# Turning keys and queries by VectorE block transposes and DMAs through DRAM, from step 13 on, in a DeltaNet and hardswish kernel

## The chip, the cores and the metric

The kernel runs on one core of a Trainium2 chip. The metric is the time of one execution in microseconds (us) on the device. A core has five engines that each work through a queue of their own in order: TensorE (PE; its weight loads are listed apart as PEld), VectorE (DVE), ScalarE (ACT), GpSimd (POOL) and SyncE (SP, which here only sends DMAs). They wait for each other by semaphores.

## The reference

Two stages. The first is a recurrence over 768 tokens for 4 batches and 8 heads of width 48, the second a two-layer network over the 3072 rows that come out of it. All is in float32.

```python
def _attn_ref(q, k, v, beta):                     # (4, 8, 768, 48)
    k_n = k / (np.linalg.norm(k, axis=-1, keepdims=True) + 1e-06)
    state = zeros((B, H, D, D))
    for t in range(S):
        y[:, :, t] = einsum('bhd,bhde->bhe', q[:, :, t], state)
        v_old = einsum('bhde,bhd->bhe', state, k_n[:, :, t])
        state = state + beta[:, :, t] * einsum('bhd,bhe->bhde', k_n[:, :, t], v[:, :, t] - v_old)
    return y
def _moe_ref(x, w_in, w_out):                     # (3072, 384), (384, 2048), (2048, 384)
    h = x @ w_in
    g = h * np.clip(h + 3.0, 0.0, 6.0) / 6.0
    return g @ w_out
```

## The kernel before

**Chunks and steps.** The 768 tokens are cut into N = 24 chunks of C = 32. A tile of 128 partitions holds one chunk of all four batches (32 rows a batch). Each chunk t is one step of the recurrence, and has three kinds of work:

- The preparation `prep(t)`: GpSimd multiplies the keys by their inverse norms (`kb`, L510). TensorE turns keys and queries, four 128x128 transposes each, into PSUM (`pt`, L524), in which heads lie two by two, padded from 48 to 64 columns. ScalarE evicts them into one tile (`KQ`, L532) that has the head's width along the partitions. GpSimd makes a mask (`mb`, L486). TensorE multiplies keys by keys and queries (`sc`, L547, 64 small matmuls), and VectorE writes the products with the mask (`L` and `LB`, L558). GpSimd scales the keys by beta (`bkb`, L498).
- The inverse of a lower triangular matrix for each chunk, for four chunks at a time, on VectorE (`A`, `pr`, L759 and L764, many short instructions; block transposes at L469 and L473).
- The chain `chain(t)`: the state times `KQ` (`ks`, L806), the residual `R` (L901, L909), `pz` and `py` (L827), the state's update (`su`, L938; `state`, L956), and the output row turned for the second stage (`yt`, L873; `xT`, L877). The chain of t + 1 needs the state of t.

**The second stage** works on blocks of two chunks (256 rows). First comes the up product with the gate: 16 units by the plain product (`ph`, L994; gate L1001 and L1004) for early blocks, or, from block 5 on, by a scheme with fewer products (`up_by_eleven`: `ph`, L1066; GpSimd's sums L1030; ScalarE's L1080, L1100, L1104; VectorE's L1093, L1097, L1107), for which VectorE first makes sums over tokens (L1056). Then comes the down product, from block 2 on with seven products in the place of eight (`po`, L1218; sums L1204; ScalarE's L1225; adds L1228), 14 units. At its end eight DMAs store the block's rows (`out_dram`, L1143).

**Order.** Every engine's order is that in which the program issues the instructions. A list by hand (`ORDER`) sets it for the start, steps 0 to 4. From step LS = 5 on, a loop does one step per turn and cuts it into 15 units. In each unit it first runs what a table `plan` holds for that unit (a piece of the chain or of a preparation), then issues `loads`, then one unit of the second stage, then some pieces of the inverse (`fill`); how many is worked out from an estimate of VectorE's load (`USED`, `CHAIN`). The second stage's 30 units per block are two steps, so the same unit of a block falls on the same place in every second step; the stores are issued in unit 11 of the odd steps. Whenever the loop is at step t, the preparation of t + 6 is being done (fewer ahead in the first two turns, called `behind`), and the one of t + 7 is begun:

```python
                1: lambda: (take(ch), take(now)),
                2: lambda: (take(ch), take(now), take(gens["q"], 4)),
                4: lambda: (take(ch), take(now)),
                5: lambda: take(now),
                6: lambda: take(now),
                13: lambda: take(later),
```

Here `now` is the preparation of t + 6 and `later` that of t + 7; `take(x)` lets it run to its next `yield`. So `kb` is made in unit 13 of the step before, the keys are turned in unit 1, the queries in unit 2, and `sc` comes in unit 4.

**SyncE's queue.** All loads and stores of these steps are sent by SyncE in program order: four `vf` loads (L193) at the beginning of a step, four `qb` loads (L180) in unit 2, two `kf` loads (L168) per unit in some steps, and the stores. Each of these has 48 KB. A send whose buffer isn't free, or whose data isn't ready, keeps all sends behind it waiting.

**Buffers.** PSUM has four banks for `pt`, `ph`, `po`, `pz`, `py` and `yt` in a ring ("pm"), and two pairs for `ks`, `su` and `sc`. There are two buffers for `kb`, four for `qb`, six for `KQ`. The tile `o` of the stores (one buffer) is also used by ScalarE's L1104.

Of the kernel before, what the change touches and what calls it, by code (L numbers as in the profile page):

```python
# [9 lines left out]
FP32 = mybir.dt.float32  # L10
# [34 lines left out]
def kernel(  # L45
# [21 lines left out]
    nc = tc.nc  # L67
# [27 lines left out]
    def rows(b):  # L95
        return slice(C * b, C * b + C)
# [20 lines left out]
    mb_spare = spares[:, 8 * H * C : 10 * H * C]  # L117
    bkb_spare = spares[:, 10 * H * C : 10 * H * C + H * DP].rearrange("p (h w) -> p h w", w=DP)
    assert 10 * H * C + H * DP == 3 * NPR * P
    kbufs = [persist.tile([P, H, DP], FP32, name=f"kb{i}") for i in range(NKB)]  # L120
    qbufs = [persist.tile([P, H, DP], FP32, name=f"qb{i}") for i in range(NQB)]
    bkbufs = [bkb_spare] + [
        persist.tile([P, H, DP], FP32, name=f"bkb{i}") for i in range(1, NBKB)
    ]
# [1 line left out]
    def bkb_of(t):  # L126
        return bkbufs[t if t < NBKB else 1 + (t - 1) % (NBKB - 1)]
# [3 lines left out]
    def tokens(ap, b, t):  # L131
        return ap[b, :, t * C : (t + 1) * C, :].rearrange("h t d -> t h d")
# [4 lines left out]
    def needs(*what):  # L137
        assert past.issuperset(what), (what, set(what) - past)
# [33 lines left out]

    def load_q(t, eng=nc.sync):
        if t < N:
            if t >= NQB:
                needs(("qT", t - NQB))
            elif t:
                needs(*pad(t))
            for b in range(B):
                eng.dma_start(out=qbufs[t % NQB][rows(b), :, 0:D], in_=tokens(q, b, t))  # L180
                if b == B - 1:
                    past.add(("q", t))
                yield
# [310 lines left out]
    def scaled(t):  # L494
        needs(("kb", t), *pad(t), *([("bkb", t - NKB)] if t >= NKB else []))
        if t >= NBKB:
            needs(("su", t - NBKB + 1))
        nc.gpsimd.tensor_tensor(  # L498
            out=bkb_of(t)[:, :, 0:D], in0=kbufs[t % NKB][:, :, 0:D],
            in1=beta_tok[:, t, 0:H].unsqueeze(2).to_broadcast([P, H, D]), op=ALU.mult,  # L500
        )
        past.add(("bkb", t))
        yield

    def prep(t, whole=True):

        g, i = group(t)
        kb, qb = kbufs[t % NKB], qbufs[t % NQB]
        needs(*([("bkb", t - NKB)] if t >= NKB else []), *(pad(t) if t < NKB and t else []))
        nc.gpsimd.tensor_tensor(  # L510
            out=kb[:, :, 0:D], in0=kfs[g][:, i],
            in1=invs.pop(t).unsqueeze(2).to_broadcast([P, H, D]), op=ALU.mult,
        )
        past.add(("kb", t))
        yield

        for j, src in enumerate((kb, qb)):
            if j == 1:
                needs(("q", t))
                past.add(("qT", t))  # L520
            ring("pm", NPM, ("pt", t, j))
            pt = psM.tile([128, NP, P], FP32, name="pt", tag=slot["pm"])
            for p in range(NP):
                nc.tensor.transpose(  # L524
                    pt[:, p, :], src[:, 2 * p : 2 * p + 2].rearrange("p e w -> p (e w)"), ident[:]
                )
# [5 lines left out]
            nc.scalar.activation(  # L532
                out=KQ[:, :, 0:4:3, :] if j == 0 else KQ[:, :, 1:3, :],
                in_=pt[:].rearrange("q p (x y c) -> q (p x) y c", y=2, c=C), func=ACTF.Copy,
            )
            if whole and j == 0:
                drain(mask(t))
            yield
        ring("pc", NPC, ("sc", t))
        sc = psC.tile([P, 2, 512], FP32, name="sc", tag=slot["pc"])  # L540
        scv = sc[:, :, 0 : NP * 2 * C].rearrange("p e (a j w) -> p e a j w", a=NP, j=2)
        for p in range(NP):
            for b in range(B):
                for e in range(2):
                    r = slice(DP * e, DP * e + DP)
                    kq = KQ[r, p * B // 2 + b // 2]
                    nc.tensor.matmul(  # L547
                        scv[rows(b), e, p],
                        lhsT=kq[:, 3 if b % 2 else 0, :],
                        rhs=kq[:, 3:1:-1, :] if b % 2 else kq[:, 0:2, :],  # L550
                        start=True, stop=True,
                    )
# [12 lines left out]
        if whole:  # L565
            drain(scaled(t))
        yield
# [219 lines left out]
    def chain(t, whole=True):  # L787
# [10 lines left out]
        def of_state():  # L798
            ph = [banks("ks", t, i) for i in range(2)]
            for p in range(NP):  # L800
                for b in (0, 2, 1, 3):
                    for e in range(2):
                        r = slice(DP * e, DP * e + DP)
# [622 lines left out]
    with tc.manual_schedule():  # L1426
# [11 lines left out]
        loads = iter(())  # L1438
        left = due = 0
        USED = {"up": 0.42, "eleven": 1.0, "down": 0.7}  # L1440
        CHAIN = {0: 0.45, 1: 0.75, 2: 0.75, 3: 0.4, 4: 0.4, 6: 0.5, 9: 0.8, 10: 0.6, 14: 0.2}
        for t in range(LS, N):
            g, i = group(t)
# [9 lines left out]
            if i == 2:  # L1453
# [12 lines left out]
                11: lambda: token_sums(t // CB),  # L1466
                13: lambda: take(later),
            }
            if behind:
                for u in (7, 8, 10, 11, 12, 13):  # L1470
                    plan[u] = lambda ch=plan.get(u): (ch and u < 13 and ch(), take(more))
                plan[14] = lambda: take(later)
            ready = (2, 0) if behind or i == 2 and t - LS == LA - LE else (1, 6)
            for u in range(NU):
                if u in plan:
                    plan[u]()
                take(loads, 2)
# [12 lines left out]
                settle(1)  # L1490
                while evicts:
                    evicts.pop(0)()
                if i == 1 == ready[0] and 5 < u < 7:
                    continue
                if i == 0 or not left:
                    take(fill, 2 if i or u < 2 else u > 4)
                    continue
                room = max(1.65 - USED[mode["of"]] - CHAIN.get(u, 0), 0.15) / mode["mean"]
                due += room * left / max((GS - i) * NU - u, 1)
                due = min(due, 2.6)  # L1500
                take(fill, int(due))
                left, due = max(left - int(due), 0), due - int(due)
# [33 lines left out]
```

## Time and profile before

| what | value |
|---|---|
| median of 3 runs | 667.27 us (665.14 to 668.17) |
| profiled execution | 672.08 us, span of its instructions 670.4 us |
| PE busy | 636.9 us, 95% |
| DVE busy | 487.2 us, 73% |
| ACT busy | 272.8 us, 41% |
| POOL busy | 203.6 us, 30% |
| granted TensorE clock, mean | 0.985 of full speed |
| memory traffic | 26.84 MB read, 4.72 MB written |

The profile is of one execution. Its page gives the busy time of each engine, the span in 40 slices, the chain of work that ended last, and the costliest groups of instructions as "line, engine, operation, out<-in, shapes, count | busy us, mean ns of one | idle time before them, and what ended it". Other views cut it by stage (windows), by line or tile, or list the instructions in order of time. The page says this of the end's chain:

```profile
PE 86%; DMA 5%; DVE 3%; SPq 2%; issue 1%; ACT 1%; POOL 0%; ACTq 0%; DVEq 0%; POOLq 0%
```

### The profile page before, as it was taken

The page shows a single profiled execution, that of the slowest core. Times are in us where ns is not written, and L with a number is a line of the kernel's source. Part 1 is how long each engine was busy: PE and PEld are TensorE (multiplying, and loading weights), DVE is VectorE, ACT ScalarE, POOL GpSimd, SP SyncE. Part 2 cuts the span into 40 slices and gives each one's busy share as a digit, 9 for nine tenths or more (in the row PEclk, how much of TensorE's full clock was granted, in tenths as well). Part 3 has the DMA queues.
Part 4 walks back from the last instruction along what each step waited for, and adds up shares of the span by engine and source line. Part 5 has one row for each costly group of instructions (what it writes and reads, how often), then busy time and mean ns, then how long its engine had stood idle before and what let it go on. Part 6 is the DMA issues. An engine that isn't in the chain of part 4 may idle for free.

```text
span 670.4 us, 26330 instructions
## 1 busy us (share of the span) xinstructions
PE 636.9 (95%) x11544; PEld 568.6 (85%) x11544; DVE 487.2 (73%) x1146; ACT 272.8 (41%) x532; POOL 203.6 (30%) x320
## 2 busy tenths in 40 slices
PE   2768899999999999999999999999999999999997
PEld 2657786776688988988989999999999999999997
DVE  4889685899545777747879847988748988556354
ACT  5887568532142232232234234235244144153250
POOL 5531022002421031364155255055042141331330
PEclk9959899999999999999999999999999999999999
DMA  7888237302041030032030020020020020010000
GB/s 171 203 193 235 59 67 186 73 6 51 15 80 32 2 72 2 3 73 37 3 68 8 3 61 14 3 62 2 3 50 2 2 49 2 17 24 2 25 1 25
DMA packets 88499, 33.27 MB, mean 50 GB/s; under 512 B 80160, under 2 KB 83232, under 8 KB 88384
## 3 DMA queue, kind: packets, MB, share of 16 engines
q1 hardware_dynamic: 88128, 31.29, 20.7%
q8 instruction: 91, 1.49, 0.9%
q10 hardware_dynamic: 256, 0.30, 0.2%
q14 instruction: 24, 0.20, 0.1%
HBM read 26.84 MB, written 4.72 MB: 47 GB/s over the span
## 4 chain that ended last, share of the span: by engine, by line
PE 86%; DMA 5%; DVE 3%; SPq 2%; issue 1%; ACT 1%; POOL 0%; ACTq 0%; DVEq 0%; POOLq 0%
PE po L1218 28%; PE ph L1066 20%; PE ph L994 15%; PE po L1154 6%; PE ks L806 3%; PE su L938 3%; PE pz L827 3%; PE py L827 3%; PE pt L524 2%; PE sc L547 2%; DMA spare<-in_moe_w_in_dram 2%; DMA kf<-in_k_dram 1%; PE yt L873 1%; DMA w_out<-in_moe_w_in_dram 1%; PE pi L684 1%
## 5 line engine op out<-in xcount | busy, mean ns | idle before, releaser
L1066 PE MATMUL ph<-xT,w_in 128*128 128x128 f32 (+1 forms) x560 | 121.4, 321 | 0.8 <-ACT KQ L532 0.6
L994 PE MATMUL ph<-xT,w_in 128*128 128x256 f32 (+1 forms) x576 | 116.6, 351 | 2.9 <-DVE g L1004 2.1
L1218 PE MATMUL po<-w_out,g 128*128 128x192 f32 x640 | 110.6, 326 | 0.0
L994 PEld LDWEIGHTS ph<-xT,w_in 128*128 128x128 f32 x576 | 94.5, 192 | 15.8 <-DVE g L1004 2.9
L1218 PEld LDWEIGHTS po<-w_out,g 128*128 128x128 f32 x640 | 104.6, 190 | 0.5
L1066 PEld LDWEIGHTS ph<-xT,w_in 128*128 128x128 f32 x560 | 91.1, 191 | 6.0 <-ACT KQ L532 0.8
L1030 POOL TENSOR_TENSOR g<-g 128x256 f32<-128x256 f32 x112 | 68.0, 608 | 83.2 <-ACT g L1080 78.8
L1218 PE MATMUL po<-spare,g 128*128 128x192 f32 x480 | 86.7, 332 | 0.0
L1218 PEld LDWEIGHTS po<-spare,g 128*128 128x128 f32 x480 | 77.2, 190 | 1.8
L1001 ACT ACTIVATE g<-ph,halves 128x256 f32<-128x256 f32 (+1 forms) x96 | 41.3, 436 | 74.9 <-PE ph L994 74.8
L1080 ACT ACTIVATE g<-ph 128x512 f32<-128x512 f32 x56 | 33.4, 597 | 82.1 <-PE ph L1066 82.1
L1228 POOL TENSOR_TENSOR o<-o,u 128x192 f32<-128x192 f32 x18 | 13.2, 733 | 175.7 <-ACT o L1225 97.2
L1204 DVE TENSOR_TENSOR g<-g 128x512 f32<-128x512 f32 x80 | 55.6, 716 | 5.6 <-PE po L1218 5.6
L759 DVE TENSOR_TENSOR pr<-A 128x30 f32<-128x30 f32 (+9 forms) x150 | 57.4, 383 | 2.8
L764 DVE TENSOR_TENSOR A<-A,pr 128x30 f32<-128x30 f32 (+9 forms) x150 | 55.7, 371 | 3.7
L1004 DVE SCALAR_TENSOR_TENSOR g<-g,ph 128x256 f32<-128x256 f32 (+1 forms) x96 | 34.8, 371 | 31.7 <-ACT g L1001 31.4
L356 ACT ACTIVATE spare<-spare,places 128x768 uint16<-128x768 uint16 (+1 forms) x56 | 52.4, 942 | 2.7 <-DMA kf<-in_k_dram 1.5
L1093 DVE TENSOR_TENSOR g<-ph,g 128x256 f32<-128x256 f32 x56 | 23.5, 420 | 38.4 <-PE ph L1066 30.9
L1225 ACT ACTIVATE o<-po 128x192 f32<-128x192 f32 x40 | 13.2, 330 | 83.2 <-PE po L1218 79.6
L510 POOL TENSOR_TENSOR kb<-kf,inv 128x384 f32<-128x384 f32 x24 | 21.3, 891 | 78.8 <-issue 42.6
L1154 PE MATMUL po<-w_out,g 128*128 128x384 f32 x128 | 45.2, 491 | 0.0
L1107 DVE SCALAR_TENSOR_TENSOR g<-o,g 128x512 f32<-128x512 f32 x56 | 40.7, 726 | 5.9 <-ACT o L1104 5.9
(141 smaller groups left out, 1010.6 us busy)
## 6 DMA issues: line engine op xcount, KB each, us to landing
kf<-in_k_dram SPq DMA_DIRECT2D x96, 48.0 KB, 2.9
qb<-in_q_dram SPq DMA_DIRECT2D x96, 48.0 KB, 2.8
vf<-in_v_dram SPq DMA_DIRECT2D x96, 48.0 KB, 2.2
out_dram<-o SPq DMA_DIRECT2D x92, 48.0 KB, 1.6
spare<-in_moe_w_in_dram SPq DMA_DIRECT2D x4, 768.0 KB, 6.0
w_out<-in_moe_w_in_dram SPq DMA_DIRECT2D x4, 768.0 KB, 6.5
w_out<-in_moe_w_out_dram SPq DMA_DIRECT2D x4, 768.0 KB, 7.3
spare<-in_moe_w_out_dram SPq DMA_DIRECT2D x4, 768.0 KB, 5.7
```

What stands on the lines that cost most here:

```text
L356: nc.scalar.activation(out=z, in_=z if n else d.bitcast(I16)[:, :, :, 3], func=func, bias=places[:, n : n + 1], scale=scale,)
L759: nc.vector.tensor_tensor(out=pv, in0=A[:, j + 1 :, j].unsqueeze(2).to_broadcast([n, w, j]), in1=A[:, j, 0:j].unsqueeze(1).to_broadcast([n ...
L764: nc.vector.tensor_tensor(out=A[:, j + 1 :, 0:j], in0=A[:, j + 1 :, 0:j], in1=pv, op=ALU.subtract)
L827: nc.tensor.matmul(ps[rows(place(b)), D * h : D * h + D], lhsT=m(h)[rows(b)], rhs=z[rows(b), D * at(h) : D * at(h) + D], start=True, stop= ...
L994: nc.tensor.matmul(ph[:, cols], lhsT=w_in[:, s, f * 128 : (f + 1) * 128], rhs=xT[:, s, cols], start=(s == 0), stop=(s == NKT - 1),)
L1001: nc.scalar.activation(out=g, in_=ph, func=ACTF.Relu, bias=half, scale=1.0 / 6.0)
L1030: nc.gpsimd.tensor_tensor(out=out, in0=a, in1=b, op=op)
L1066: nc.tensor.matmul(ph[:, n], lhsT=w, rhs=x, start=start, stop=stop, skip_group_check=True)
L1107: nc.vector.scalar_tensor_tensor(out=g, in0=r, scalar=1.0, in1=g, op0=ALU.min, op1=ALU.mult)
L1154: nc.tensor.matmul(pos[c][:], lhsT=gs[blk, f // 2][:, f % 2, c * P : (c + 1) * P], rhs=w_out[:, f, :], start=(f == 0), stop=(f == NFC - 1),)
L1204: nc.vector.tensor_tensor(out=A(f, *out, 4), in0=A(f, *a, 4), in1=A(f, *b, 4), op=op)
L1218: nc.tensor.matmul(ps[n][:], lhsT=A(f - f % 2, *a)[:, f % 2], rhs=b[:, f], start=(f == 0), stop=(f == HF - 1),)
```

## The change

From TQ = 13 on, a preparation turns keys and queries another way. VectorE transposes the 32x32 blocks of the key tile (128 partitions x 384) and of the query tile. Each result is written to a DRAM tile `kq` by four DMAs, one per batch, in rows of 32 numbers; the address does the rest of the turning. Two DMAs, one for the even and one for the odd heads, read `kq` back into `KQ`, on 48 of each 64 partitions. For this the tiles of keys and queries lie dense from step 13 on (384 columns, no padding), and the matmuls that read `KQ` (`sc` and `ks`) take 48 rows in place of 64. The results of the block transposes (`turned`) stand in the place of two of the four query buffers, so two are left for queries.

In the table the preparation's pieces move: `kb` from unit 13 to 10, the key transpose with its four writes to unit 11, the query transpose with its four writes to unit 12, the two reads and the mask to unit 1 of the next step; `sc` stays in unit 4 and what follows in unit 5. For step 13's own preparation the pieces lie in units 12 to 14 of step 6. The estimate of VectorE's load has 0.75 more in units 11 and 12 (`TURN`).

```diff
-    qbufs = [persist.tile([P, H, DP], FP32, name=f"qb{i}") for i in range(NQB)]
+    TQ, HQ = LS + 2 * LE, 2
+    qb_pair = persist.tile([P, HQ, H, DP], FP32, name="qbs")
+    qbufs = [persist.tile([P, H, DP], FP32, name=f"qb{i}")[:] for i in range(NQB - HQ)] + [
+        qb_pair[:, i] for i in range(HQ)
+    ]
+    turned = qb_pair[:].rearrange("p i h w -> p (i h w)")[:, 0 : 2 * H * D].rearrange(
+        "p (k z) -> p k z", k=2
+    )
...
     def load_q(t, eng=nc.sync):
         if t < N:
-            if t >= NQB:
-                needs(("qT", t - NQB))
+            if q_before(t) is not None:
+                needs(("qT", q_before(t)))
...
+        if t >= TQ:
+            kq = scratch.tile([H * D, B // 2, 4, C], FP32, name="kq", bufs=2)
+            for j, src in enumerate((of_key(t), of_query(t))):
+                if j == 1:
+                    needs(("q", t))
+                    past.add(("qT", t))
+                nc.vector.transpose(out=turned[:, j], in_=src.rearrange("p h w -> p (h w)"))
+                for b in range(B):
+                    nc.sync.dma_start(
+                        out=kq[:, b // 2, (3 if j == 0 else 2) if b % 2 else j, :].rearrange(
+                            "(n r) c -> r n c", r=C
+                        ),
+                        in_=turned[rows(b), j].rearrange("p (n c) -> p n c", c=C),
+                    )
+                yield
+            ring("KQ", NKQ, ("KQ", t))
+            KQ = work.tile([128, NP * B // 2, 4, C], FP32, name="KQ", bufs=NKQ)
+            for e in range(2):
+                nc.sync.dma_start(
+                    out=KQ[DP * e : DP * e + D].rearrange("d (p x) y c -> d p (x y c)", p=NP),
+                    in_=kq[:].rearrange("(p e d) x y c -> e d p (x y c)", e=2, d=D)[e],
+                )
+            drain(mask(t))
+            yield
-        for j, src in enumerate((kb, qb)):
+        for j, src in enumerate((kb, qb) if t < TQ else ()):
...
-                    r = slice(DP * e, DP * e + DP)
+                    r = slice(DP * e, DP * e + (DP if t < TQ else D))
...
+        TURN = {11: 0.75, 12: 0.75}
...
+            if first_of >= TQ:
+                plan[2] = lambda: (take(ch), take(gens["q"], 4))
+                plan[6] = lambda: None
+            if first_of + 1 >= TQ and not behind:
+                plan[10] = lambda: (take(ch), take(later))
+                plan[11] = lambda: (token_sums(t // CB), take(later))
+                plan[12] = lambda: take(later)
+                plan[13] = lambda: None
...
+                if first_of + 2 == TQ:
+                    plan[12] = plan[13] = lambda: (take(more), take(later))
+            turns = TURN if first_of + 1 >= TQ else {}
...
-                room = max(1.65 - USED[mode["of"]] - CHAIN.get(u, 0), 0.15) / mode["mean"]
+                room = max(1.65 - USED[mode["of"]] - CHAIN.get(u, 0) - turns.get(u, 0), 0.15) / mode["mean"]
```

More of the change, by code (lines that the diff above doesn't have):

```diff
@@ L119, with of_key, of_query, dense @@
     assert 10 * H * C + H * DP == 3 * NPR * P
-    kbufs = [persist.tile([P, H, DP], FP32, name=f"kb{i}") for i in range(NKB)]
-    qbufs = [persist.tile([P, H, DP], FP32, name=f"qb{i}") for i in range(NQB)]
+    kbufs = [persist.tile([P, H, DP], FP32, name=f"kb{i}")[:] for i in range(NKB)]
+    TQ, HQ = LS + 2 * LE, 2
[6 more added lines that the diff above has]
+    )
+    def of_key(t):
+        return dense(kbufs[t % NKB], t)
+    def of_query(t):
+        return dense(qbufs[t % NQB if t < TQ else t % (NQB - HQ)], t)
+    def dense(x, t):
+        if t < TQ:
+            return x[:, :, 0:D]
+        return x.rearrange("p h w -> p (h w)")[:, 0 : H * D].rearrange("p (h w) -> p h w", w=D)
+    def q_before(t):
+        slot = [s % NQB if s < TQ else s % (NQB - HQ) for s in range(t + 1)]
+        return max((s for s in range(t) if slot[s] == slot[t]), default=None)
     bkbufs = [bkb_spare] + [
@@ L179, in load_q @@
             for b in range(B):
-                eng.dma_start(out=qbufs[t % NQB][rows(b), :, 0:D], in_=tokens(q, b, t))
+                eng.dma_start(out=of_query(t)[rows(b)], in_=tokens(q, b, t))
                 if b == B - 1:
@@ L498, in scaled @@
         nc.gpsimd.tensor_tensor(
-            out=bkb_of(t)[:, :, 0:D], in0=kbufs[t % NKB][:, :, 0:D],
+            out=bkb_of(t)[:, :, 0:D], in0=of_key(t),
             in1=beta_tok[:, t, 0:H].unsqueeze(2).to_broadcast([P, H, D]), op=ALU.mult,
@@ L510, in prep @@
         nc.gpsimd.tensor_tensor(
-            out=kb[:, :, 0:D], in0=kfs[g][:, i],
+            out=of_key(t), in0=kfs[g][:, i],
             in1=invs.pop(t).unsqueeze(2).to_broadcast([P, H, D]), op=ALU.mult,
@@ L802, in of_state @@
                     for e in range(2):
-                        r = slice(DP * e, DP * e + DP)
+                        r = slice(DP * e, DP * e + (DP if t < TQ else D))
                         c = slice(2 * C * (b // 2), 2 * C * (b // 2) + 2 * C)
```

## The prediction

> **What bounds the kernel now.** I read the page first: busy shares and clock.
>
> ```profile
> PE 636.9 (95%) x11544; PEld 568.6 (85%) x11544; DVE 487.2 (73%) x1146; ACT 272.8 (41%) x532; POOL 203.6 (30%) x320
> ...
> PEclk9959899999999999999999999999999999999999
> ```
>
> TensorE is busy 95% of the span, at full granted clock after the start. A busy share is a mean over stages, so next the busy time step by step, in windows cut at each step's first `ks` matmul (us from the span's start; then length, PE, PEld, DVE, ACT, POOL).
>
> ```profile
> 342.20:368.00 25.80, 25.20 (x467) 22.82 (x467) 22.09 (x52) 12.62 (x26) 14.45 (x22) 1.00 0.20 40
> 393.10:418.20 25.10, 24.94 (x466) 22.93 (x465) 17.96 (x41) 12.74 (x26) 13.93 (x23) 1.00 0.22 44
> 418.20:443.30 25.10, 25.10 (x454) 23.87 (x453) 22.86 (x55) 6.10 (x13) 4.75 (x8) 1.00 0.05 12
> 516.50:539.90 23.40, 23.40 (x382) 22.33 (x381) 21.76 (x52) 4.30 (x10) 5.35 (x8) 1.00 0.05 13
> ```
>
> These are steps 12, 14, 15 and 19. The steps in which the changed preparation lies (7 to 17) are full of matmuls; step 12 alone lacks 0.6 us. So a matmul taken away there is time gained, and a wait put on TensorE there is time lost. Step 19, with no preparation left, is 1.7 us shorter than step 15: that is what a preparation costs. The chain of waits in steps 14 and 13 splits it:
>
> ```profile
> 370.64 0.44 PE pt L524 x4
> ...
> 395.32 0.44 PE pt L524 x4
> ...
> 397.29 0.44 PE pt L524 x4
> ...
> 400.98 0.79 PE sc L547 x53
> ```
>
> Four transposes hold TensorE for 0.44 us; `sc`, which stays, for 0.79. Last, SyncE's queue and VectorE at the turn from step 13 to 14 (it starts at 393.15), where the new work goes (start, us):
>
> ```profile
> 389.31 0.28 DVE L1056 TENSOR_TENSOR beta_tok<-xT,beta_tok 128x128 f32<-128x128 f32 x1
> 390.07 4.63 SPq L1143 DMA_DIRECT2D out_dram<-o  x8
> 394.74 1.90 SPq L193 DMA_DIRECT2D vf<-in_v_dram  x4
> 396.74 2.33 SPq L180 DMA_DIRECT2D qb<-in_q_dram  x4
> 400.91 0.86 PE L547 MATMUL sc<-KQ 64*32 64x64 f32 x64
> ```
>
> Out of steps 7, 9, 11, 13 and 15 come eight output stores; sending them takes SyncE 3.58 to 4.63 us (mean of the five batches 3.9), a batch of four 48 KB loads 1.86 to 3.12 (nineteen batches of `vf` and `qb`: mean 2.15, with the gap behind it 2.2).
>
> **What goes.** Preparations 13 to 23 lie in steps 7 to 17 (the first one's start in step 6). Each loses 8 transposes, 2 x 0.44 = 0.88 us of TensorE; 11 x 0.88 = 9.7. In step 12 TensorE also waits for ScalarE's `KQ` eviction to free a PSUM bank:
>
> ```profile
> L1066 PE MATMUL ph<-xT,w_in 128*128 128x128 f32 (+1 forms) x560 | 121.4, 321 | 0.8 <-ACT KQ L532 0.6
> ```
>
> That goes too. I take 0.7: 10.4 us gained in all. The 22 evictions (0.60 us each) leave ScalarE, 41% busy; nothing more is won by that.
>
> **What comes, costed at nothing.** 22 VectorE transposes of 128x384. Rows for 256 and 768 columns:
>
> ```profile
> L702 DVE STREAM_TRANSPOSE sums_in<-sums_in 128x256 f32<-128x256 f32 x4 | 1.8, 445 | 0.4
> L255 DVE STREAM_TRANSPOSE beta_tok<-spare 128x768 f32<-128x768 f32 x1 | 1.0, 970 | 0.0
> ```
>
> On the line between them 384 columns take 0.445 + 128 x (0.970 - 0.445)/512 = 0.576 us, 12.7 us in all, on an engine 63 to 91% busy in these steps, while the schedule draws about as much filler work off units 11 and 12 (`TURN`). Cover gone, the gate multiplies behind them (L1093), which free `ph` banks, come late: at most 0.58 a step. GpSimd's `kb` multiply (0.83 us) moves from unit 13 to 10, past the four L1228 adds or two pairs of gate adds; GpSimd stands idle 5.13 us before those adds, so it is early. Without that cover VectorE would wait for it, and all sends behind. `q` has two buffers instead of four, but its loads (unit 2) lead their use (unit 12) by ten units, some 17 us. The mask stays at unit 1.
>
> **What comes, with a price: the sends.** Each preparation puts 8 writes (384 pieces of 128 bytes each) and 2 reads (192 pieces of 1 KB each) on SyncE, in the program's order. In an odd step the order becomes: the four key writes (unit 11, behind the token sums L1056 and the transpose), the eight stores (that unit's), the four query writes (unit 12), four `vf` loads (next step, unit 0), the two reads (unit 1, waiting for all writes to land), and behind that wait four `qb` loads, which nobody needs soon. `sc`, at unit 4, waits for the reads, and everything on TensorE behind it.
>
> A send's cost isn't shown for these shapes. It was the same 0.42 to 0.45 us for the 32 pieces of a store and the 256 of a load, so I take a load batch's mean, 2.2 us; from below 1.9 (quickest batches), from above 1.5 times (by pieces), 3.3. Landing: 48 KB loads take
>
> ```profile
> qb<-in_q_dram SPq DMA_DIRECT2D x96, 48.0 KB, 2.8
> vf<-in_v_dram SPq DMA_DIRECT2D x96, 48.0 KB, 2.2
> out_dram<-o SPq DMA_DIRECT2D x92, 48.0 KB, 1.6
> spare<-in_moe_w_out_dram SPq DMA_DIRECT2D x4, 768.0 KB, 5.7
> ```
>
> A 196 KB read lies between 1.9 (quickest `vf`) and 5.7; nearest to the small ones: 2.5 us.
>
> Steps 12, 14, 16 (numbers of 14): the token sums end at 389.6; transpose to 390.2; key writes sent by 392.4; stores by 396.3; query writes by 398.5; `vf` by 400.7 (the query writes have landed: last sent at 398.0 + 1.6); second read sent from 401.2, landed 403.7. `sc` stood at 400.91, 0.88 earlier now: 400.0. TensorE waits 3.7, three times: 11.1.
>
> Steps 8, 10: no token sums yet, so the key transpose (after L1228 at 233.80) ends at 235.0, key writes by 237.2, the stores were ready at 236.80. Then 241.1, 243.3, 245.5, second read at 246.0, landed 248.5 against 247.7: 0.8 each, 1.7 with step 10's longer stores.
>
> Step 7: both transposes lie at the end of step 6, behind a gate multiply that ends at 213.3; eight writes by 218.3, four `vf` and two `kf` loads by 221.6, second read landed 224.6 against 222.1: 2.5.
>
> Steps 9, 11, 13, 15, 17: no stores in the way; in step 15 the query transpose comes behind L1107 and one filler, by 417.1; writes 419.3, `vf` 421.5, landed 424.5 against 425.5. In time, with 1.0 to spare; zero.
>
> Stores later by the key writes' 2.2 also hold up ScalarE's L1104, which rewrites their buffer: up to 1 us in steps 12, 14, 16 if `sc` weren't waiting; beneath its wait, nothing.
>
> **Sum:** 11.1 + 1.7 + 2.5 = 15.3 lost, 10.4 gained: +4.9. The profiled execution took 672.08 (span 670.4), 0.7% above the median 667.27; the difference goes onto the median: **672 us**. With quickest batches (1.9, stores 3.6, landing 2.0) the losses are 3 x 1.9 + 0.9 = 6.6, net -3.8; with Q and K batches of 3.3 these six steps lose 2.2 more each, the five odd ones 0.1: +18.6. This case spans 664 to 686.
>
> **Rivals.** *The reads come in time* (faster). Its place is SyncE between the key writes and the reads: 22 sends. The quickest single send in these steps is 0.34 us; at 0.38 with its gap the 22 take 8.4, the second read lands 390.2 + 8.4 + 2.0 = 400.6: 0.6 late in three steps, net -8.6; with none late -10.4: 657 to 663. It decides at about 0.36 a send. For it: the sends' own time is all that spaces these batches, and an engine that got them quicker would shed the whole delay. Against it: no batch of loads or stores went below 0.45 a send.
>
> *Small pieces are slow.* The load on the engines:
>
> ```profile
> q1 hardware_dynamic: 88128, 31.29, 20.7%
> ```
>
> 0.207 x 16 x 670.4 us / 88128 = 25 ns a piece. A write has 24 pieces an engine: 0.60 us, hidden behind the sends. If writing 128 bytes to DRAM costs twice that, four writes take 4.8 and land 1.6 after: the reads in 14 are sent at 402.7 and land at 405.7 (5.7 late), in 8 and 10 2.8 late, in 7 6.0, in the five others 1.0: 33.7 - 10.4 = +23, 690 us. The nearest row against it: nothing here writes pieces under 1536 bytes, and those stores land soonest of all.
> [...]
>
> *VectorE becomes late.* In steps 12 and 16 it is busy over 22 of 25 us. If each step's two transposes reach TensorE whole, 12.7 are lost, and with reads in time 12.7 - 10.4 gives 669.6. Against it: L1093 has idle time before it at unit 11.
>
> **Chances.** Late reads as summed 0.50; in time 0.25; slow pieces 0.13; VectorE 0.12. A difference under 0.5% (3.3 us) can't be told from none. Faster: the second case, 0.25. Same: the lower part of the first (0.13) and most of the last (0.08). Slower: the rest, 0.54. The range 658 to 686 leaves out the slow pieces and the bottom of the second case, 0.19 together; the likeliest case alone has 664 to 686.
>
> **What would show it.** TensorE waiting at `sc` L547 for `KQ` from a DMA: 3 to 4 us in steps 12, 14, 16, under 1 in 8 and 10, 2.5 in 7, none in 9 to 17 odd; 88 of the 192 `pt` transposes gone; 22 transposes near 0.58 us; SyncE's order as above. The prediction is wrong if `sc` finds `KQ` ready, if the reads are late in odd steps too (slow pieces), or if waits appear at `ph` behind L1093.

## The result, and the profile after

The changed kernel takes 698.88 us (median of 4 runs, 695.26 to 707.05); the kernel before took 667.72 us beside it (4 runs, 665.14 to 672.91). The ratio is 1.044, 95% interval 1.035 to 1.053 (without the run of 707.05, whose mean granted clock was 0.941, where the others had 0.960 to 0.963). So it is slower, by 31.2 us of these medians and by 29.9 without that run, and the forecast of 672 us with its range of 658 to 686 was wrong. The profiled execution after took 700.18 us (span 698.5).

The page of the changed kernel: the busy time of TensorE is nearly what it was, its share fell, and the clock line has three slices at 8 behind the start, where the one of before has 9 throughout.

```profile
PE 638.1 (91%) x11456; PEld 567.5 (81%) x11456; DVE 495.9 (71%) x1168; ACT 260.0 (37%) x510; POOL 202.1 (29%) x320
...
PEclk9769999999999989999989999998999999999999
```

The windows of steps 12, 14 and 15 of the changed kernel (start and end in us, length, busy time of PE, PEld, DVE, ACT, POOL, granted clock, DMA share, GB/s):

```profile
349.30:381.30 32.00, 27.04 (x460) 24.57 (x459) 21.66 (x52) 11.27 (x23) 13.25 (x21) 0.89 0.28 51
407.00:437.20 30.20, 25.73 (x459) 23.52 (x458) 18.66 (x42) 11.65 (x25) 13.19 (x22) 0.94 0.30 56
437.20:461.40 24.20, 24.20 (x446) 23.02 (x445) 23.03 (x54) 4.85 (x11) 6.48 (x9) 1.00 0.28 48
```

Step 15, in which nothing is late, went from 25.1 to 24.2 us: that is the 0.9 us which the removed transposes were to bring. Step 12 went from 25.8 to 32.0 and step 14 from 25.1 to 30.2. They lack busy time (5.0 and 4.5 us of their length), and TensorE's granted clock in them is 0.89 and 0.94. The same cut through all steps from 7 to 21 gives 371.7 us before and 402.1 after, 30.4 more. So the whole loss lies there.

What TensorE waited for in these steps (the waits of the changed kernel; us in total, times, longest):

```profile
PE sc L593 <- DMA KQ<-kq: 17.5, 12, 3.3
PE pz L873 <- DVE R L955: 5.0, 4, 2.0
PE pz L873 <- DVE X L495: 3.4, 3, 2.2
```

One wait of `yt` for `y` in step 20 (0.8 us) comes to it. By step, the `sc` line is 2.5 us in step 7, 2.5 and 1.9 in 8 and 10, and 4.0, 3.8 and 2.7 in 12, 14 and 16, two waits in each step, since each of the two reads is waited for by its own half of `sc`. The `R` line is 1.0, 0.6 and 2.0 in steps 12, 14 and 16, and 1.4 in step 13. The `X` line is 0.7, 2.2 and 0.5 in steps 9, 17 and 21. That makes 26.7 us. Less the 10.4 us gained, 16.3 of the 30.4 are explained so far.

SyncE's queue at the turn from step 13 to 14 (start and length in us; step 14 starts at 407.0):

```profile
404.00 1.86 SPq L547 DMA_DIRECT2D kq<-qbs  x4
405.96 4.27 SPq L1189 DMA_DIRECT2D out_dram<-o  x8
410.33 1.92 SPq L547 DMA_DIRECT2D kq<-qbs  x4
412.30 1.96 SPq L215 DMA_DIRECT2D vf<-in_v_dram  x4
414.43 0.81 SPq L557 DMA_DIRECT2D KQ<-kq  x2
```

The order is the one forecast, and so are the times of the sends, counted from the step's start: the stores are out at 3.2 us, the query writes at 5.3, `vf` at 7.3, the reads at 8.2. The chain of waits then has 3.96 us from the second read's send to `sc`, not 2.5. The page's DMA list gives the landings of the new transfers (KB each, median us from issue to landing), and the list of groups the new transposes (busy us, mean ns):

```profile
kq<-qbs SPq DMA_DIRECT2D x88, 48.0 KB, 1.8
KQ<-kq SPq DMA_DIRECT2D x22, 192.0 KB, 3.9
```

```profile
L545 DVE STREAM_TRANSPOSE qbs<-qb 128x384 f32<-128x384 f32 x11 | 6.3, 572 | 0.0
```

What is left of the 30.4 us lies in the clock. Two windows of the changed kernel, during the wait in step 14 and just behind it:

```profile
415.50:418.90 3.40, 0.37 (x14) 0.24 (x21) 0.93 (x3) 0.00 (x0) 0.00 (x0) 1.00 0.96 172
418.90:422.30 3.40, 3.40 (x73) 3.23 (x73) 0.76 (x2) 0.39 (x1) 0.00 (x0) 0.51 0.03 5
```

TensorE does 0.37 us of work in the first, and then, with work without a gap, runs at half speed in the second. The trace of the clock has such stretches at half in steps 7, 8, 12, 14, 16 and 17, each 3.4 or 6.8 us long, 30.7 us together. Not all of that is work: in steps 8, 12 and 16 a stretch begins while TensorE still waits, as here in step 12 (2.73 us of work in 3.40), and these waits are counted above already.

```profile
360.90:364.30 3.40, 2.73 (x69) 2.56 (x70) 0.76 (x2) 0.00 (x0) 0.00 (x0) 0.50 0.22 31
```

TensorE is busy for 27.0 of the 30.7 us. In them its 128x192 matmuls start 0.32 us apart, at full clock 0.16 (medians, 200 to 640 us); `sc` takes 1.07 us in step 14, at half clock, and 0.86 in step 15. If all this work loses half of its time, as those matmuls do, that is 13.5 us (an estimate; by `sc` it is a little high). With the waits and the gain this makes 26.7 + 13.5 - 10.4 = 29.8, against the 30.4 of the steps. Before the change there is no half clock between 76 and 670 us.

### The profile page after: what moved, and what is told of

It reads as the page before. It is cut to its first block, busy times and chain, and to the rows that moved or that the text cites. A ratio compares the mean times of both kernels' runs of the same rounds, so it can differ in the third digit from the quotient of the medians.

```text
span 698.5 us, 26278 instructions
## 1 busy us (share of the span) xinstructions
PE 638.1 (91%) x11456; PEld 567.5 (81%) x11456; DVE 495.9 (71%) x1168; ACT 260.0 (37%) x510; POOL 202.1 (29%) x320
## 4 chain that ended last, share of the span: by engine, by line
PE 68%; DVE 15%; SPq 6%; DMA 5%; issue 4%; ACT 1%; POOL 0%; DVEq 0%; ACTq 0%; POOLq 0%
PE po L1264 20%; PE ph L1112 14%; PE ph L1040 13%; PE po L1200 6%; DMA KQ<-kq 3%; PE sc L593 3%; PE su L984 2%; DVE A L810 2%; PE pz L873 2%; PE py L873 2%; PE ks L852 2%; DVE pr L805 2%; PE pt L570 2%; SPq L547 2%; DVE g L1153 2%
## 5 line engine op out<-in xcount | busy, mean ns | idle before, releaser
L1112 PE MATMUL ph<-xT,w_in 128*128 128x128 f32 (+1 forms) x560 | 123.9, 328 | 0.0
L1040 PEld LDWEIGHTS ph<-xT,w_in 128*128 128x128 f32 x576 | 96.2, 194 | 16.2 <-DVE g L1050 2.2
L1112 PEld LDWEIGHTS ph<-xT,w_in 128*128 128x128 f32 x560 | 94.2, 197 | 5.8 <-issue 0.5
L1264 PEld LDWEIGHTS po<-spare,g 128*128 128x128 f32 x480 | 79.4, 194 | 1.9 <-issue 0.2
L1126 ACT ACTIVATE g<-ph 128x512 f32<-128x512 f32 x56 | 33.4, 596 | 96.3 <-PE ph L1112 96.3
L810 DVE TENSOR_TENSOR A<-A,pr 128x30 f32<-128x30 f32 (+9 forms) x150 | 55.8, 372 | 3.3
L805 DVE TENSOR_TENSOR pr<-A 128x30 f32<-128x30 f32 (+9 forms) x150 | 55.7, 371 | 2.9
L1050 DVE SCALAR_TENSOR_TENSOR g<-g,ph 128x256 f32<-128x256 f32 (+1 forms) x96 | 34.6, 370 | 31.0 <-ACT g L1047 30.4
L593 PE MATMUL sc<-KQ 64*32 64x64 f32 (+1 forms) x1536 | 25.7, 252 | 26.1 <-DMA KQ<-kq 17.5
L593 PEld LDWEIGHTS sc<-KQ 64*32 64x32 f32 (+1 forms) x1536 | 19.7, 119 | 32.6 <-issue 19.7
```

Of the source, the lines that this page charges most:

```text
L593: nc.tensor.matmul(scv[rows(b), e, p], lhsT=kq[:, 3 if b % 2 else 0, :], rhs=kq[:, 3:1:-1, :] if b % 2 else kq[:, 0:2, :], start=True, sto ...
L805: nc.vector.tensor_tensor(out=pv, in0=A[:, j + 1 :, j].unsqueeze(2).to_broadcast([n, w, j]), in1=A[:, j, 0:j].unsqueeze(1).to_broadcast([n ...
L810: nc.vector.tensor_tensor(out=A[:, j + 1 :, 0:j], in0=A[:, j + 1 :, 0:j], in1=pv, op=ALU.subtract)
L1040: nc.tensor.matmul(ph[:, cols], lhsT=w_in[:, s, f * 128 : (f + 1) * 128], rhs=xT[:, s, cols], start=(s == 0), stop=(s == NKT - 1),)
L1112: nc.tensor.matmul(ph[:, n], lhsT=w, rhs=x, start=start, stop=stop, skip_group_check=True)
L1264: nc.tensor.matmul(ps[n][:], lhsT=A(f - f % 2, *a)[:, f % 2], rhs=b[:, f], start=(f == 0), stop=(f == HF - 1),)
```

## The experiments

My theory after the result: the loss has three parts, late reads, a late inverse, and the half clock that TensorE's waits bring on. Rivals were that the clock falls for another reason of the changed kernel, that `TURN` is harmless, and that the late stores, not the reads, set the end. The times of the kernel before beside these runs were 667.7 to 670.95 us (medians of 7 to 27 runs).

### Is it the waits that halve the clock?

Two kernels ask this from both sides. The first puts useless matmuls in front of `sc`, about as long as its waits:

```diff
+        for _ in range({13: 6, 14: 6, 16: 5, 18: 8, 20: 8, 22: 7}.get(t, 0)):
+            nc.tensor.matmul(sc[:, 0, 256:512], lhsT=w_in[:, 2, 0:128], rhs=w_in[:, 2, 0:256], ...)
         for p in range(NP):
```

> The changed kernel with useless 128x256 matmuls on TensorE before sc in the steps where it waits: 6, 6, 5, 8, 8, 7 of them in steps 7, 8, 10, 12, 14, 16, 0.43 us each, 17 us in all, into a part of the PSUM tile that nobody reads. Theory (the idle stretches at sc make the granted clock fall to half for the 3.4 to 6.8 us that follow, 27 us in these steps): the wait at sc is filled, the clock stays up, and the kernel gets faster by about 10 us though it computes more, 685 to 692 us. Rival (the fall of the clock has another cause or costs nothing): as long as the changed kernel or up to 17 us longer, 698 to 716 us.

Measured: 696.26 us, ratio 1.035 (1.028 to 1.041), between the two ranges. `sc` waits 1.9 us instead of 17.5, and half clock in steps 7 to 21 is 3.4 us instead of 30.7. So the median, 2.6 us below the changed kernel's, decides nothing, but steps 7 and 8 do: with matmuls in the place of the waits they take 27.8 and 27.5 us at full clock, with the waits 29.3 and 30.5. More work made them shorter. Six useless matmuls take 2.86 us in step 7, so the 40 of them take some 19 us (an estimate), as much as the waits that they fill and more; that is why the whole kernel gains so little. Its line for `sc`:

```profile
PE sc L598 <- DMA KQ<-kq: 1.9, 4, 0.7
```

The second takes the kernel before, with nothing of the change, and makes `sc` wait in the odd steps, by a chain of one, two or three small copies of `R`:

```diff
+        hops = {15: 1, 17: 2, 19: 2, 21: 3, 23: 2}.get(t, 0)
+        src = hops and latest[-1][:, 0:16]
+        for n in range(hops):
+            late = work.tile([P, 16], FP32, name=f"late{n}", bufs=1)
+            nc.sync.dma_start(out=late[:], in_=src)
+            src = late[:]
+        if hops:
+            nc.tensor.matmul(sc[0:16, 0, 256:272], lhsT=src, rhs=src, ...)
```

> The kernel before, with nothing of the change, but with waits put ahead of sc in the odd steps: R is copied through one, two or three small transfers in a row (step 9: one; 11, 13 and 17: two; 15: three), and one small extra matmul that reads the last copy stands ahead of sc; nothing is left out. Each hop takes some 2 us, R is ready 1.7 us ahead of sc: TensorE waits about 0.5, 2.5, 2.5, 4.5 and 2.5 us, 12 in all. My theory: the wait alone takes the clock to half, with no transfer of keys in the program: 3.4 to 6.8 us of half clock behind each wait of 2.5 us or more, none behind the short one, and the time is 12 us plus half of some 20 us above before: 685 to 697 us. Rival: the half clock in the changed kernel came from something else of it (its transfers, its 48-row matmuls); then the clock stays full here and the time is before's plus the waits: 679 to 684.

Measured: 699.42 us, ratio 1.046 (1.039 to 1.052), above both ranges. The waits of this kernel behind two or three copies, and two windows, of the shortest wait (step 9) and what follows it:

```profile
PE sc L550 <- DMA late<-late: 18.4, 4, 6.1
```

```profile
273.90:277.30 3.40, 1.59 (x70) 1.50 (x71) 1.02 (x3) 0.00 (x0) 1.21 (x1) 1.00 0.05 7
277.30:280.70 3.40, 3.40 (x13) 3.40 (x12) 2.68 (x6) 0.00 (x0) 1.33 (x2) 0.51 0.00 0
```

The waits came out longer than I had worked out (20.9 us with the 2.5 behind a single copy, not 12), even the shortest took the clock to half, and behind the five there are 23.9 us at half, in which TensorE is busy for 21.8. 20.9 + 10.9 = 31.8; the steps 7 to 21 took 32.1 us more than in the kernel before. The expected sizes were off, but the theory holds and its rival falls: this program has no turned keys, and its clock falls all the same. A wait on TensorE cost itself and up to 3.4 us more here.

### Is TURN harmless?

The room that `TURN` takes from the inverse was costed at nothing. One kernel empties it in the changed kernel, another puts the same 0.75 us into the kernel before:

```diff
-            turns = TURN if first_of + 1 >= TQ else {}
+            turns = {}
```

> The changed kernel with TURN empty: the schedule takes no filler work off units 11 and 12. Theory (the estimate pushes the end of the inverse into units 0 to 2 of steps 9, 13 and 17, so pz waits for X there): the waits of pz in 9, 13, 17 (1.1, 1.7, 2.5 us) and the small ones in 20 and 21 (1.1, 0.9) go, with the slow clock of step 17 (3.4 us at half, 1.7): 9 us faster than the changed kernel, 690 us. Rival (the two transposes themselves make VectorE late): those waits stay, 697 to 702 us. The waits at sc in steps 7 to 16 stay in both.

```diff
+                later_turn = 0.75 if first_of + 1 >= 13 and u in (11, 12) else 0
-                room = max(1.65 - USED[mode["of"]] - CHAIN.get(u, 0), 0.15) / mode["mean"]
+                room = max(1.65 - USED[mode["of"]] - CHAIN.get(u, 0) - later_turn, 0.15) / mode["mean"]
```

> The kernel before, with one thing of the change: in units 11 and 12 of every step from 7 on, the share of the block inverse (VectorE's filler) is reduced by the 0.75 us that the change's table TURN sets aside, with no transposes and no DMAs added; nothing is left out. My theory: the inverse then ends later, in units 0 to 2 of the next step, its last product X comes late, and pz waits for it in steps 9, 13, 17 and 21 for 0.9 to 2.5 us each: 5 to 8 us more than before in all, 672 to 679. Rival: with VectorE's transposes absent the room is made up elsewhere and X is in time: within 1.5 us of the kernel before.

Measured: the first 696.62 us, ratio 1.036 (1.028 to 1.045), not told apart from the changed kernel. `pz` waits 0.2 us for `X` instead of 3.4, but 6.7 instead of 5.0 for `R`, and the half clock grew to 34.1 us: the late `X` went, as the theory had it, but the 9 us did not come. The second 677.17 us, ratio 1.009 (1.005 to 1.013), 7.2 us above before, within my range; TensorE waits in it for `X` 1.4 us (steps 17 and 21, not 9 and 13), for `y` 1.4 (steps 12 and 16) and for `R` 0.9 (step 20), none of which it did before. In its trace steps 7 to 21 are 4.5 us longer than before, and the stretch ahead of step 7, which the edit leaves as it was, 1.9 us for no cause that shows.

So `TURN` alone costs 0.5 to 1.3% by the interval: less filler in units 11 and 12 means more of it at the end of a group of four, in front of `X`, `y` and `R`. Its share in the changed kernel is not settled by the first run, since the other waits and the clock moved with it.

### What makes the reads late?

Three kernels move sends. The first sends the four `vf` loads behind the two reads, the second moves the key writes of odd steps behind the stores, the third sends the writes from ScalarE's queue:

```diff
-            take(gens["v"], 4)
+            if first_of < TQ:
+                take(gens["v"], 4)
...
-                plan[2] = lambda: (take(ch), take(gens["q"], 4))
+                plan[2] = lambda: (take(ch), take(gens["v"], 4), take(gens["q"], 4))
```

> The changed kernel with the four vf loads sent behind the two KQ reads (unit 2) and not before them, from step 7 on. Theory (sc waits for the sends that stand before the reads in SyncE's queue): the reads go out 2.0 us sooner where the queue is what they wait for; the waits at sc in steps 7, 8, 10, 12, 14, 16 shrink by up to 2.0 each (at most 12 in all), and the clock falls to half less often: 676 to 688 us. Rival (the reads wait for the writes' landing or the DMA engines are the limit): no sooner, 696 to 701 us.

```diff
-                plan[11] = lambda: (token_sums(t // CB), take(later))
-                plan[12] = lambda: take(later)
+                plan[11] = lambda: (token_sums(t // CB), None if t % 2 else take(later))
+                plan[12] = lambda: take(later, 1 + t % 2)
```

> The changed kernel, but in the odd steps both transposes and all eight writes of key and query are issued in unit 12, behind the eight output stores, and not four of them ahead of the stores; nothing is left out. My theory: the queue has the same 22 transfers ahead of the two reads in either order, so sc waits as long in steps 8, 10, 12, 14 and 16 (some 11 to 15 us in all with step 7), while the stores go out as early as before the change and the three waits of pz for R in steps 12, 14 and 16 (1.0 to 2.3 us each) go; time that pz no longer waits, sc waits instead, since the reads land at the same moment. So the time stays within 3 us of the changed kernel: 696 to 702. Rival: the late stores add their own time to that of the late reads; then it falls by their 4.7 us and by what the clock loses after them, to 688 to 693.

```diff
-                    nc.sync.dma_start(
+                    nc.scalar.dma_start(
                         out=kq[:, b // 2, (3 if j == 0 else 2) if b % 2 else j, :]...
```

> The changed kernel with one edit: the eight writes of key and query to DRAM are issued from ScalarE's queue, not from SP's; nothing is left out. On SP, stores, loads of v and the two reads of the next turn stay in their order, so the stores go out as before the change and the reads wait for 8 sends less. My theory: sc's waits in steps 8 to 16 go (step 7's may stay), pz no longer waits for late stores in 12, 14 and 16, and the clock stays full there; the late X of TURN in steps 9, 13, 17 remains, and ScalarE's 8 issues of 0.47 us a step delay its evictions by at most 2 us where o is on the path: 674 to 682 us. Rival: the issues on ScalarE (3.8 us a step) hold up o and y, and VectorE behind them, by more than the reads gain: 690 or above.

`vf` behind the reads: 693.41 us, ratio 1.032 (1.025 to 1.038). `sc`'s waits fall from 17.5 to 10.7 us, half clock from 30.7 to 20.5. The place was right, but I had expected 676 to 688: a batch of four is only part of what is late, and `R` and `X` are late as before (5.2 and 3.5 us).

Key writes behind the stores: 707.24 us, ratio 1.054 (1.048 to 1.060). Both the theory (no change) and its rival (a gain) fell; it is slower by 8 us of medians. `sc`'s waits, and SyncE's queue out of step 13, which here starts at 388.2:

```profile
PE sc L593 <- DMA KQ<-kq: 25.7, 12, 4.9
```

```profile
410.84 3.58 SPq L1189 DMA_DIRECT2D out_dram<-o  x8
414.52 5.49 SPq L547 DMA_DIRECT2D kq<-qbs  x8
```

The stores go out 22.6 us into the step, as their data come; in the changed kernel the key writes went out at 22.7 and the stores at 24.7. In step 9 the key writes went out while the queue had nothing else to send, and the stores started 21.8 us into the step all the same (21.9 here). So the same number of sends does not mean the same time: before the stores are ready a send is free, behind them it is not. And the late stores' 2.4 us at `pz` came back at `sc`: in steps 12, 14 and 16 the waits for `R` and at `sc` together are 14.1 us in the changed kernel and 15.1 here, though those for `R` fell from 3.6 to 1.2. The end there is set by the reads' landing, as I had thought; the late stores' waits lie within it. Most of the rest of `sc`'s rise, 4.4 us, lies in steps 8 and 10.

Writes from ScalarE: 702.36 us, ratio 1.051 (1.041 to 1.061). The reads are hardly late any more (`sc` waits 3.1 us in all), and the time is lost on ScalarE's queue, as the rival had it, though at `g` and not at `o` or `y`. The waits, and ScalarE's queue in step 11:

```profile
PE ph L1112 <- ACT g L1126: 15.1, 3, 5.9
```

```profile
340.52 6.22 ACTq L547 DMA_DIRECT2D kq<-qbs  x8
346.79 1.09 ACT L1126 ACTIVATE g<-ph 128x512 f32<-128x512 f32 x2 [9.44 <-DMA kq<-qbs]
```

Eight sends stand ahead of the eviction L1126 that frees a `ph` bank, each takes 0.78 us while SyncE sends the stores, and TensorE waits 5.9 us.

### A better order

If the waits are the loss, an order without them should bring the 10 us. The first try does `kb`, both transposes and the writes in units 5, 7 and 8 of every step, where SyncE has little to send, with `vf` behind the reads and `TURN` empty:

```diff
-                plan[10] = lambda: (take(ch), take(later))
-                plan[11] = lambda: (token_sums(t // CB), take(later))
-                plan[12] = lambda: take(later)
+                plan[5] = lambda: (take(now), take(later))
+                plan[7] = lambda: take(later)
+                plan[8] = lambda: (take(ch), take(later))
...
-            turns = TURN if first_of + 1 >= TQ else {}
+            turns = {}
```

> The changed kernel with kb, key and query transposes and the writes in units 5, 7 and 8 in place of 10, 11 and 12 (ahead of the token sums and stores), the vf loads behind the reads, and TURN empty. Theory (the whole loss is the place of these pieces in SyncE's queue, its result at the clock, and TURN): no wait at sc or pz, stores as early as before, and the 10.4 us of the transposes are won: 655 to 661 us, faster than the kernel before. Rival (the block transposes on VectorE or the DMA traffic cost by themselves): 667 us or more.

Measured: 669.58 us, ratio 0.998 (0.994 to 1.001). The clock is full, `sc` waits 0.8 us for a read, but the gain isn't there; VectorE is late with `y` in steps 12, 14 and 16, where `yt` waits for it for 4.6 us in all. The rival's range held, 667 us or more.

The second does this in odd steps alone and leaves the even ones in units 10 to 12; the third is the second from step 14's keys on:

```diff
+                if t % 2:
                     plan[5] = lambda: (take(now), take(later))
...
+                else:
                     plan[10] = lambda: (take(ch), take(later))
```

```diff
-    TQ, HQ = LS + 2 * LE, 2
+    TQ, HQ = LS + 2 * LE + 1, 2
```

> The changed kernel put in another order, nothing left out: in odd steps (those with the output stores) kb, the two transposes and the eight writes are issued in units 5, 7 and 8, in even steps in units 10 to 12 as the change has them; the four loads of v go out behind the two reads; TURN is empty. My theory: sc is in time in every step but 7 (whose late read is not touched), y of steps 12, 14 and 16 is not pushed back by early transposes as in e6_early_turns (there 5.7 us of waits of yt), and the clock stays at full speed; 11 turns that TensorE no longer makes bring 0.9 us each: 663 to 666 us. Rival: where VectorE makes the transposes in units 11 and 12, the inverse or the next step is late again, and the gain stays lost: 668 to 674.

> The same as e7_early_in_odd, but the new way begins with step 14's key and query, not with step 13's, so that step 7, in which the first late read falls, is as before the change; nothing is left out. My theory: step 7 is 0.8 us shorter than in e7 (1.8 us of waits go, 0.9 us of TensorE's turn comes back): 662 to 665 us. Rival: the first read in the new way is as late in step 8 as it was in step 7, and the time is e7's or up to 1 us above.

Measured: 668.28 us, ratio 0.997 (0.994 to 1.000), and 669.21 us, ratio 1.000 (0.996 to 1.003). The second is the best of all runs, 1.7 us by medians, at the edge of what can be told from none, and both are above what I had expected; the third is no better than the second. In the second steps 8, 10, 11, 12 and 14 take 23.9 to 24.7 us, 0.8 to 1.8 less than before the change. What it still loses is 1.5 us at `sc` in step 7, 1.4 at `po` for no cause that shows, and this:

```profile
PE pz L873 <- DVE R L955: 3.4, 4, 1.4
```

These and 0.2 us at `X` are 6.5 us of waits, against 10.4 gained; its steps 7 to 21 are 2.8 us shorter than before. The waits for `R` lie in steps 13 and 15 to 17; in 13 and 17, which have 2.7 of the 3.4 us, `R` stands behind the last block transpose of the inverse on VectorE. That transpose in step 13, before the change (step 13 starts at 368.0) and in this kernel (at 362.5), from VectorE in order of time:

```profile
370.89 1.98 DVE L473 STREAM_TRANSPOSE X<-A 128x1024 f32<-128x1024 f32 x1
```

```profile
366.67 1.98 DVE L495 STREAM_TRANSPOSE X<-A 128x1024 f32<-128x1024 f32 x1
```

Before the change it starts 2.9 us into the step, here 4.2. In steps 7 to 12 VectorE is busy 120.6 of 149.1 us here, and was 116.4 of 153.2: the steps got shorter, its work longer. So I took VectorE, with its order of work, for the next bound. Two kernels test that by dealing the inverse out earlier, over the units that are left less 6 or less 12:

```diff
-                due += room * left / max((GS - i) * NU - u, 1)
+                due += room * left / max((GS - i) * NU - u - 6, 1)
```

> e7_early_in_odd with one edit: the pieces of the block inverse are dealt out over the units that are left less 6, so that its last product X comes at unit 11 of steps 12, 16 and 20, not at unit 14 or in the next step; nothing is left out. My theory: what e7 still loses is VectorE's work of the last step before a new inverse is used (20.0 us busy in the 25.7 us of step 13, and pz waits 1.7 us there and 1.6 in step 17), and an earlier end takes back 3 us of it: 664 to 666 us. Rival: VectorE is full from step 10 to 12 already, and the same wait only moves to y, yt or R of steps 11, 12, 15 and 16: 667 to 670.

> The same with 12 units, X at unit 8 or 9 of steps 12, 16 and 20. My theory: pz waits in steps 13 and 17 are gone, but the denser filler in steps 10, 11, 14 and 15 pushes R or y back there by some 0.5 to 1 us each; 664 to 668 us, no better than e9. Rival: VectorE has enough room in these steps, and it is a further 1 us faster than e9.

Measured: 668.90 us, ratio 1.002 (0.999 to 1.005), and 674.79 us, ratio 1.010 (1.006 to 1.013). With 6, `pz`'s waits for `R` fall to 1.4 us, and waits for `y` (1.1 at `yt`, and 1.1 at `pz` for ScalarE's), `g` (1.2) and `xT` (0.4) take their place. With 12, `R` is late in steps 12 to 20 for 6.9 us, and its wait in step 12 brings 3.4 us of half clock. The rival held for 6, and for 12 it was worse than either. The wait moves, mostly between VectorE's results; it doesn't go.

## Why the prediction was wrong

**What held.** The two sides of the sum were the right ones: transposes off TensorE, 0.9 us in step 15, where nothing is late (25.1 to 24.2), and 0.6 in step 11, against SyncE's queue. `sc` waited for its reads in the six steps named and in no odd step but 7. The sends came within 0.3 us of the times worked out for step 14. The transposes took 0.572 us, 0.576 was read off the line. The rival of slow pieces did not happen: the four writes of 128-byte pieces took 1.9 us to send and landed in 1.8, no later than the loads (2.1 and more). In the trace a piece of 128 bytes took 12 ns, one of the loads' 192 bytes 15 (medians, 205 to 500 us); the rival needed 50. That a write of 128 bytes costs twice the 25 ns was an assumption, and no run shows it. 690 us and more was reached all the same, by another way.

**First step that failed: "nearest to the small ones: 2.5 us".** The reads landed in 3.9 us (3.1 to 4.0). That is 1.4 us in every step that waits. The two reads of a step are in flight together, 384 KB, and with the `qb` loads behind them they keep the DMA engines busy for 96% of the window of 415.50 above. On the line between the prediction's own rows, 48 KB in 1.9 us and 768 KB in 5.7, 384 KB would take 3.7 (an estimate; no run sent one read alone). Steps 12, 14 and 16 lost 5.0, 4.4 and 4.7 us (with `R`'s waits, which lie ahead of the same landing), not 3.7 each, and steps 8 and 10 lost 2.5 and 1.9, not 0.8 each; step 7 lost 2.5 as forecast, by luck: its second read was sent 1.1 us earlier into the step than worked out and landed 1.4 later. Together it is 21.0 us against 15.3. The bounds, 1.9 and 5.7, held the true value, and the one taken lay at the wrong end.

**Second step that failed: `TURN` and the transposes "costed at nothing".** The cover was named as filler drawn off units 11 and 12. The filler isn't free: the inverse must be done when `R` of the next group needs it. `X`, `R` and `y` were late in steps 9, 13, 17, 20 and 21 for 5.6 us together. The price given for the case that the cover is gone was put on the gate multiplies L1093, where no wait came. The kernel before with `TURN` alone, 7.2 us slower, shows that this step costs by itself; how the 5.6 us divide between `TURN` and the transposes stays open, since with `TURN` empty waits of 1.0 and 1.3 us for `R` are left in steps 13 and 17. The rival "VectorE becomes late" had the engine right, and most of the waits left in the better order are for VectorE.

**What the sum did not hold at all: the clock.** The windows of before showed 1.00 in every step, and I took TensorE's speed as given. Each wait was priced at its own length. The 27.0 us of work at half clock lost another 13.5 (the estimate above), half of the whole error: 4.9 forecast + 5.7 (reads) + 5.6 (VectorE) + 13.5 (clock) = 29.7, against 29.9 to 31.2 measured. The kernel before with waits put in has the same half clock (23.9 us of it), and the kernel whose waits are filled with matmuls has 3.4 us of it.

The step on the stores, that their delay lies beneath `sc`'s wait and costs nothing, looked wrong in the waits (3.6 us at `R` in steps 12, 14 and 16) and was right by the run that sent them early: what `pz` no longer waited for there, `sc` did.

## What to carry to other kernels

A wait put on TensorE where it is never idle is to be priced with its clock: here 2 to 5 us of waiting within a step mostly brought 3.4 or 6.8 us at half speed behind it. Work that is moved onto a filler's time costs when the filler has a due date (7.2 us here for `TURN` alone), so look for who needs the filler's last result, not at the engine's busy share. And a send ahead of one that isn't ready yet was free here, while one behind it pushed what came after: in step 9 the stores started 21.8 us into the step with the key writes ahead of them and 21.9 without, and with those writes behind them the reads went out 2.3 us later, counted from that step's start.

## What the runs showed of the hardware that I had not expected

**The clock went by fixed windows.** In the traces before and after, all changes of the granted clock lie on a grid of 3.413 us that runs on through the execution, and the clock is full or half. I divided both traces along their grids and took TensorE's busy share from its matmuls, for the windows at full clock between 200 and 640 us. Of the 120 of the changed kernel six were followed by half clock, those busy for 7.9, 12.0, 34.9, 37.0, 42.4 and 55.1%; the 114 others, busy for 57.2% or more, were not, and none of the 129 of the kernel before was, all busy for 82.5% or more. So it mattered how waits fell on the grid: of the two in step 7, 1.6 and 0.9 us, 1.5 us lie in one window (the one of 55.1%), and the clock fell; the two in step 10, 1.2 and 0.7 us, fall on two windows, 68 and 76% busy, and it did not. Of the nine windows at half clock between 200 and 640 us, three, busy for 25.4, 80.6 and 90.9%, were followed by another, and six, busy for 94.5% or more, by full clock: so the stretches in steps 8, 12 and 16 came to 6.8 us. In the first 80 us the busy share alone doesn't divide them: windows at full clock of 31.6 and 49.3% were followed by full clock, others of 55.8 and 58.3% by half, and windows at half clock of 83.5 and 84.4% by full.

**A read of 192 KB from DRAM in pieces of 1 KB, with a second one in flight, took 3.1 to 4.0 us to land** in the changed kernel, with medians of 3.7 to 3.9 in seven of its variants, while the writes of 128-byte pieces landed in 1.8.

**Left open.** In step 17 of the three better orders TensorE stands 1.1 to 1.6 us at `po` or `sc` for nothing that the profile shows ("issue"). No data transfer is in flight then; in each of the three traces a transfer of 16 KB on the queue that the page calls "instruction" ends 1.3 to 1.5 us before TensorE goes on. Whether it waited for that was not tested.
